# A 2:4-pruned linear layer on one core: a 256-column first weight piece, nine staged tiles in the place of ten, and a new order of the opening

## The chip, the cores and the metric

The kernel runs on one core of a Trainium2 chip. The metric is device time in microseconds (us); smaller is better. Three runs of the kernel before gave 234.03, 234.43 and 234.66 us, a median of 234.43.

## The reference

`x` is [16, 512, 1024], `w` [1024, 1024], `b` [1024], all bf16. In each group of four consecutive rows of `w`, separately for each column, the two entries of largest magnitude are kept and the others are set to zero; then `x` is multiplied with the pruned `w`, and `b` is added:

```
wg = w.reshape(256, 4, 1024); mag = abs(wg)
thr = second largest of mag in each group of four
wp = (wg * (mag >= thr)).reshape(1024, 1024)
out = einsum("bsd,df->bsf", x, wp) + b
```

The 8192 tokens make 64 tiles of 128 tokens. A tile needs 16 matmuls of 128 x 128 by 512 columns: eight slices of the inner dimension (K) for each of the two halves of the output columns.

## The kernel before

**Two ways to feed TensorE (PE).** In the main loop (lines 291 to 313) everything is at hand: the pruned weights lie in `wp_nat[h]` (h is the half of the output columns) in eight K slices in natural order, and tokens come transposed by a DMA transpose (`issue_batch`, lines 214 to 221, tiles `xTs` and `xTb`). Each tile takes 16 matmuls at line 301, and VectorE (DVE) adds the bias out of PSUM at line 207; a pair of tiles is stored at line 313. The batches are of 2, 4, and then 8 tiles.

Until the weights are pruned and laid out so, the first T = 10 tiles are worked on in pieces; this is the opening, and the change lies in it. For the first half of K (g = 0) the kernel uses the weights as they are loaded, four rows of a group side by side on a partition (`w_gh`), and transposes the tokens on PE in the matching order. For the second half (g = 1) it uses `xg1`, a DMA transpose of the second half of the T tiles' columns, and `wp_nat`.

**The opening's order** is written out by hand in the string `FRONT` (lines 231 to 240); the loop below it (lines 242 to 270) issues each token's instructions in this order, and each engine works off its own in this order. The tokens:

- `A.i`: magnitudes of weight piece i (`abs_piece`), on VectorE (line 122) or on ScalarE (ACT, line 120). `P.i`: the piece's pruning (`prep_piece`), seven VectorE instructions, lines 133 to 143; the last writes the pruned weights.
- `W`, `w`: matmuls on zeros that keep PE at work (line 108), 512 and 128 columns wide.
- `T.t`: four PE transposes of tile t's first half (line 160); `C.t`: ScalarE's copy of them to SBUF (line 165).
- `M.i.t`: the four matmuls (line 179) of piece i and tile t. Pieces 0 to 4 belong to g = 0, pieces 5 to 7 to g = 1. `X.q.t`: four matmuls of 512 columns for tile t and quarter q = 2g + h, all of its columns at once.
- `V.h.t`: ScalarE copies a finished g = 0 sum from PSUM to a stage in SBUF (line 193). `O.h.t`: VectorE adds the g = 1 sum to the stage (line 197). `B.h.t`: VectorE adds the bias (line 201), and the tile is stored when both halves are done (line 210). The stages that have no `B` in the opening are done in the main loop, three or four a tile (lines 303 to 305).
- `U.g.h.c0.c1`, `Z.g.h.c0.c1`: four copies by DMA from `w_gh` to `wp_nat` (line 150), issued by SyncE (SP) or by ScalarE. Copy j fills K slice 4g + j, which the j-th of the four matmuls of a piece reads. `L.k`: the DMA transpose of batch k, issued by SP (line 219).

PSUM has eight banks, given out in turn (`next_bank`); a bank is free again when its `V`, `O` or bias addition has read it.

**Loads.** SP issues, in this order (lines 83 to 98): half of the first weight load (256 columns), tiles 0 and 1, the weights of columns 256 to 512, tiles 4 and 5, tiles 6 and 7, columns 512 to 1024, tiles 8 and 9, the two halves of g = 1, the bias, and the transpose `xg1`. ScalarE issues the other half of the first weight load and tiles 2 and 3. Although the first load has 256 columns, it is worked on in two pieces of 128.

The functions that the diff touches:

Of the kernel before, what the change touches and what calls it, by code (L numbers as in the profile page):

```python
# [10 lines left out]
def kernel(  # L11
# [7 lines left out]
    nc = tc.nc  # L19
    P = 128  # L20
# [5 lines left out]
    K = tc.keep_in_program_order  # L26

    B, S, D = x.shape
# [3 lines left out]
    NT = NTOK // P  # L32
    FH = 512
# [2 lines left out]
    xf = x.flatten_outer_dims()  # L36
    of = out.flatten_outer_dims()

    T = 10
    NE = 8  # L40

    const = ctx.enter_context(tc.tile_pool(name="const", bufs=1))
# [10 lines left out]
    def next_bank():  # L53
        bk = nbk[0] % 8
        nbk[0] += 1
        return bk
# [1 line left out]


    wv = w.rearrange("(g p m) f -> p g m f", g=2, m=4)  # L60
    pieces = [(0, 0, 128), (0, 128, 256), (0, 256, 512), (0, 512, 768), (0, 768, 1024),
              (1, 0, 256), (1, 256, 512), (1, 512, 1024)]
    w_gh = {(g, h): const.tile([P, 4, FH], bf16, name=f"w_{g}_{h}") for g in range(2) for h in range(2)}

    def w_of(i):
        g, c0, c1 = pieces[i]
        return w_gh[(g, c0 // FH)][:, :, c0 % FH:c0 % FH + c1 - c0]

    def load_w(g, c0, c1, eng=nc.sync, m0=0, m1=4):
        dst = w_gh[(g, c0 // FH)][:, m0:m1, c0 % FH:c0 % FH + c1 - c0]  # L70
        K(eng.dma_start(dst, wv[:, g, m0:m1, c0:c1]))  # L71
# [4 lines left out]
    def load_x(ta, tb, eng=nc.sync):  # L76
        xt = const.tile([P, tb - ta, KH], bf16, name=f"xh_{ta}")
        src = xf[ta * P:tb * P, 0:KH].rearrange("(t p) c -> p t c", p=P)
        K(eng.dma_start(xt[:], src))  # L79
        for t in range(ta, tb):  # L80
            xh[t] = xt[:, t - ta, :]
# [2 lines left out]
    load_w(0, 0, 256, nc.scalar, 2, 4)  # L84
    load_x(0, 2)
    load_x(2, 4, nc.scalar)
    load_w(0, 256, 512)
    load_x(4, 6)
    load_x(6, 8)
    load_w(0, 512, 1024)  # L90
    load_x(8, 10)
    load_w(1, 0, 512)
    load_w(1, 512, 1024)
    bias_sb = const.tile([P, Dout], bf16, name="bias_sb")
# [1 line left out]

    xg1 = const.tile([P, 4, T * P], bf16, name="xg1")
    K(nc.sync.dma_start_transpose(out=xg1[:], in_=xf[0:T * P, KH:D]))

# [7 lines left out]
    def warm(n):  # L107
        K(nc.tensor.matmul(bank[7][:, :n], lhsT=zeros[:, :P], rhs=zeros[:, :n], start=True, stop=True))  # L108
# [3 lines left out]
    def abs_piece(i, on_act):  # L112
        g, c0, c1 = pieces[i]
        n = c1 - c0
        if n <= 256:
            mag = mags_pool.tile([P, 4, n], bf16, name="mag")[:]
        else:
            mag = const.tile([P, 4, n], bf16, name=f"mag_{i}")[:]
        if on_act:
            K(nc.scalar.activation(mag, w_of(i), Act.Abs))  # L120
        else:
            K(nc.vector.tensor_single_scalar(
                mag.bitcast(u16), w_of(i).bitcast(u16), 0x7FFF, op=Alu.bitwise_and))
        mags[i] = mag

    def prep_piece(i):
        g, c0, c1 = pieces[i]
        n = c1 - c0
        mag = mags.pop(i)
        magv = mag.rearrange("p (a j) f -> p a j f", j=2)  # L130
        hi = tmp.tile([P, 2, FH], bf16, name="hi")[:, :, :n]
        lo = tmp.tile([P, 2, FH], bf16, name="lo")[:, :, :n]
        K(nc.vector.tensor_tensor(hi, magv[:, :, 0, :], magv[:, :, 1, :], op=Alu.max))  # L133
        K(nc.vector.tensor_tensor(lo, magv[:, :, 0, :], magv[:, :, 1, :], op=Alu.min))  # L134
        t1 = tmp.tile([P, FH], bf16, name="t1")[:, :n]
        t2 = tmp.tile([P, FH], bf16, name="t2")[:, :n]
        K(nc.vector.tensor_tensor(t1, hi[:, 0, :], hi[:, 1, :], op=Alu.min))
        K(nc.vector.tensor_tensor(t2, lo[:, 0, :], lo[:, 1, :], op=Alu.max))
        thr = tmp.tile([P, FH], bf16, name="thr")[:, :n]
        K(nc.vector.tensor_tensor(thr, t1, t2, op=Alu.max))  # L140
        mask = tmp.tile([P, 4, FH], bf16, name="mask")[:, :, :n]
        K(nc.vector.tensor_tensor(mask, mag, thr[:, None, :].to_broadcast([P, 4, n]), op=Alu.is_ge))  # L142
        K(nc.vector.tensor_tensor(w_of(i), w_of(i), mask, op=Alu.mult))  # L143
# [11 lines left out]
    def transpose_half(t):  # L155
        own[(0, t)] = next_bank()
        xv = xh[t].rearrange("p (q m) -> p m q", m=4)
        dst = bank[own[(0, t)]][:].bitcast(bf16)[:, :4 * P].rearrange("p (m q) -> p m q", m=4)
        for m in range(4):
            K(nc.tensor.transpose(dst[:, m, :], xv[:, m, :], ident[:]))  # L160
# [5 lines left out]
        xT[t] = xt  # L166


    def mm_part(q, t, c0, c1):
        g, h = divmod(q, 2)  # L170
        if c0 == 0 and q > 0:
            own[(q, t)] = next_bank()
        dst = bank[own[(q, t)]][:, c0:c1]
        for m in range(4):
            if g == 0:
                lhs, rhs = xT[t][:, m, :], w_gh[(0, h)][:, m, c0:c1]
            else:
                lhs, rhs = xg1[:, m, t * P:(t + 1) * P], wp_nat[h][:, 4 + m, c0:c1]
            K(nc.tensor.matmul(dst, lhsT=lhs, rhs=rhs, start=c0 == 0 and m == 0, stop=c1 == FH and m == 3))  # L179
# [34 lines left out]
    def issue_batch(t0, nb):  # L214
# [6 lines left out]
            xN[t0 + j] = xt[:, :, j * P:(j + 1) * P]  # L221


    batches = [(T, 2), (T + 2, 4)] + [(t, 8) for t in range(T + 6, NT, 8)]

# [1 line left out]


    FRONT = """
        A.0 A.1 P.0 W W W W W W W W w w T.0 T.1 C.0 T.2 T.3 C.1 P.1 w M.0.0 C.2 M.0.1 T.4 C.3 T.5 M.0.2 C.4 T.6 T.7
        A.2 M.0.3 C.5 M.0.4 P.2 M.1.0 M.1.1 C.6 M.0.5 M.1.2 C.7 M.0.6 M.1.3 M.1.4 A.3 M.0.7 M.1.5 M.1.6 M.1.7 A.4
        M.2.0 P.3 M.2.1 V.0.0 M.2.2 V.0.1 M.2.3 T.8 T.9 C.8 M.2.4 M.2.5 C.9 P.4 M.2.6 A.5 M.2.7 X.0.8 V.0.2 X.0.9
        V.0.3 V.0.4 M.3.0 P.5 U.1.0.0.256 V.0.5 M.3.1 M.3.2 V.0.6 M.3.3 V.0.7 M.4.0 M.3.4 A.6 M.3.5 M.4.1 V.0.8 P.6
        U.1.0.256.512 M.4.2 V.0.9 M.3.6 M.4.3 A.7 M.3.7 M.4.4 M.4.5 M.4.6 V.1.0 P.7 U.1.1.0.512 L.0 L.1 L.2 M.4.7
        V.1.1 X.1.8 V.1.2 X.1.9 V.1.3 M.5.0 V.1.4 M.5.1 V.1.5 M.5.2 V.1.6 M.5.3 M.6.0 V.1.7 M.5.4 V.1.8 O.0.0 M.5.5
        M.6.1 V.1.9 Z.0.0.0.512 Z.0.1.0.512 B.0.0 M.5.6 O.0.1 M.5.7 M.6.2 B.0.1 M.6.3 M.6.4 O.0.2 M.6.5 O.0.3 M.6.6
        M.6.7 O.0.4 X.2.8 O.0.5 X.2.9 O.0.6 M.7.0 O.0.7 O.0.8 M.7.1 O.0.9 M.7.2 O.1.0 M.7.3 O.1.1 M.7.4 O.1.2 O.1.3
        M.7.5 O.1.4 M.7.6 O.1.5 M.7.7 O.1.6 X.3.8 B.0.2 O.1.7 X.3.9 O.1.8 O.1.9  # L240
    """
    for tok in FRONT.split():
        k, *n = tok.split(".")
        n = [int(c) for c in n]
        if k in "Ww":
            warm(FH if k == "W" else P)
        elif k == "A":
            abs_piece(n[0], n[0] not in (0, 2))
        elif k == "P":
            prep_piece(n[0])  # L250
        elif k == "T":
            transpose_half(n[0])
        elif k == "C":
            copy_half(n[0])
        elif k == "M":
            g, c0, c1 = pieces[n[0]]
            h = c0 // FH
            mm_part(2 * g + h, n[1], c0 - h * FH, c1 - h * FH)
        elif k == "X":
            mm_part(n[0], n[1], 0, FH)  # L260
        elif k == "V":
            to_stage(*n)
        elif k == "O":
            add_stage(*n)
        elif k == "B":
            add_bias(*n)
        elif k in "UZ":
            unpack(*n, nc.sync if k == "U" else nc.scalar)
        elif k == "L":
            issue_batch(*batches[n[0]])  # L270
# [20 lines left out]
    for bi, (t0, nb) in enumerate(batches):  # L291
        if bi >= 1 and bi + 2 < len(batches):
            issue_batch(*batches[bi + 2])
        for t in range(t0, t0 + nb):
            if t == NT - 1:
                last_tile(t)
                continue
            bks = (next_bank(), next_bank())
            for kt in range(KT):
                for h in range(2):  # L300
                    K(nc.tensor.matmul(bank[bks[h]][:], lhsT=xN[t][:, kt, :], rhs=wp_nat[h][:, kt, :],  # L301
                                       start=kt == 0, stop=kt == KT - 1))
            for _ in range(4 if t == T else 3):
                if later:
                    add_bias(*later.pop(0))
            j = (t - T) % 2
            if j == 0:
                o_pair = outp2.tile([P, 2, Dout], bf16, name="o_pair")
            for h in range(2):
                evac_dve(o_pair[:, j, :], h, bks[h])  # L310
            if j == 1 or t == NT - 2:
                dst = of[(t - j) * P:(t + 1) * P, :].rearrange("(j p) f -> p j f", p=P)
                K(nc.scalar.dma_start(dst, o_pair[:, :j + 1, :]))
# [1 line left out]
_INS = ['x', 'w', 'b']  # L315
_OUTS = [((16, 512, 1024), 'bfloat16')]
# [25 lines left out]
```

## Time and profile before

| | |
|---|---|
| median of three runs | 234.43 us (234.03 to 234.66) |
| the profiled execution's own time | 234.52 us |
| its span, first to last instruction | 232.7 us |
| PE busy | 227.3 us |
| DVE, ACT busy | 117.6 us, 22.7 us |
| line 301, 128 x 512 matmuls of the main loop | 161.7 + 20.8 us |
| line 179, matmuls of the opening | 18.2 + 17.5 us |
| granted clock of PE | 1.00 |
| DMA, mean over the span | 164 GB/s |

How to read the profile: a row of the timeline gives start, length, engine, line, operation, what is written and read, shape and count, and in brackets the idle time before it and what ended it. The chain that ended last is followed back from the last instruction: at each step to what released it. A matmul's length contains its way through the array; matmuls follow one another faster than that, so what counts is the distance between their starts. "q" behind an engine's name is its sequencer, which issues DMAs. The idle time of an engine that is not on the chain costs nothing. A row of the DMA issues ends with the time from issue to landing, and the busy share of the DMA is a mean over 16 engines.

The page's busy shares in 40 slices (5.8 us each) show the opening in the first seven or eight: VectorE and ScalarE are at work nearly all the time in the first four or five, and only PE from there on.

```
PE   7999999999999999999999999999999999999995
DVE  3999898969375244234334334324424423433434
ACT  3989600000000000000000000000000000000000
DMA  6996499999989401993229932597228991122222
```

### The profile page before, as it was taken

What the parts mean: (1) busy time and instruction counts of PE and PEld (TensorE: products, weight loads), DVE (VectorE), ACT (ScalarE), POOL (GpSimd) and SP (SyncE); (2) the same over time, 40 slices, a digit from 0 to 9 for tenths busy, and PEclk for the clock granted to TensorE, in tenths of its full rate; (3) what the DMA queues carried; (4) which work ended last, traced back from release to release, by engine and by line L of the source; (5) the groups of instructions that cost most, each with busy time, mean ns of one, the idle gap of its engine ahead of it and who ended that gap; (6) DMA issues with size and microseconds to landing.
All of it is one profiled execution on the core that took longest, in us unless ns stands there. A gap on an engine that the chain in (4) does not pass through costs nothing.

```text
span 232.7 us, 2893 instructions
## 1 busy us (share of the span) xinstructions
PE 227.3 (98%) x1199; PEld 114.8 (49%) x1219; DVE 117.6 (51%) x209; ACT 22.7 (10%) x38; POOL 0.7 (0%) x6
## 2 busy tenths in 40 slices
PE   7999999999999999999999999999999999999995
PEld 3878774444444444444444444444444444444443
DVE  3999898969375244234334334324424423433434
ACT  3989600000000000000000000000000000000000
POOL 1000000000000000000000000000000000000000
PEclk9999999999999999999999999999999999999999
DMA  6996499999989401993229932597228991122222
GB/s 197 350 211 145 98 197 165 229 315 289 213 215 346 152 24 66 262 236 136 90 44 254 205 130 92 112 218 216 88 90 188 158 250 65 64 93 90 90 90 90
DMA packets 76700, 38.19 MB, mean 164 GB/s; under 512 B 61840, under 2 KB 68496, under 8 KB 76688
## 3 DMA queue, kind: packets, MB, share of 16 engines
q1 hardware_dynamic: 66192, 19.86, 47.1%
q10 hardware_dynamic: 10496, 18.16, 22.4%
q8 instruction: 9, 0.15, 0.3%
q14 instruction: 3, 0.02, 0.0%
HBM read 3.67 MB, written 16.78 MB: 88 GB/s over the span
## 4 chain that ended last, share of the span: by engine, by line
PE 95%; DMA 2%; SPq 1%; issue 1%; DVE 0%
PE bank L301 78%; PE bank L179 15%; DMA xh<-in_x_dram 2%; PE bank L276 2%; PE bank L160 1%; SPq L71 0%; SPq L79 0%; DVE o_sb L286 0%
## 5 line engine op out<-in xcount | busy, mean ns | idle before, releaser
L301 PE MATMUL bank<-wp_nat,xTb 128*128 128x512 bf16 x737 | 161.7, 379 | 0.8
L207 DVE TENSOR_TENSOR o_pair<-bank,bias_sb 128x512 bf16<-128x512 f32 x106 | 68.2, 685 | 98.0 <-PE bank L301 93.6
L301 PEld LDWEIGHTS <-xTb 128*128 128x128 bf16 x752 | 73.6, 98 | 88.7
L301 PE MATMUL bank<-wp_nat,xTs 128*128 128x512 bf16 x94 | 20.8, 379 | 0.1
L179 PE MATMUL bank<-w,xT 128*128 128x256 bf16 (+2 forms) x174 | 18.2, 262 | 0.2
L179 PE MATMUL bank<-wp_nat,xg 128*128 128x256 bf16 (+1 forms) x111 | 17.5, 318 | 0.1
L201 DVE TENSOR_TENSOR o_sb<-stage,bias_sb 128x512 bf16<-128x512 f32 x20 | 13.0, 685 | 7.3 <-DMA out_dram<-o_sb 7.2
L179 PEld LDWEIGHTS <-xT 128*128 128x128 bf16 x176 | 14.5, 98 | 3.1 <-ACT xT L165 0.3
L301 PEld LDWEIGHTS <-xTs 128*128 128x128 bf16 x96 | 9.4, 98 | 11.3
L179 PEld LDWEIGHTS <-xg 128*128 128x128 bf16 x112 | 11.0, 98 | 6.4
L197 DVE TENSOR_TENSOR stage<-bank,stage 128x512 f32<-128x512 f32 x20 | 13.0, 684 | 2.0 <-PE bank L179 1.8
L193 ACT COPY stage<-bank 128x512 f32<-128x512 f32 x20 | 10.3, 681 | 0.3 <-PE bank L179 0.3
L120 ACT ACTIVATE mag<-w 128x1024 bf16<-128x1024 bf16 (+2 forms) x6 | 6.9, 1167 | 0.4 <-DMA w<-in_w_dram 0.4
L142 DVE TENSOR_TENSOR mask<-mag,thr 128x1024 bf16<-128x1024 bf16 (+2 forms) x8 | 5.5, 692 | 0.3
L143 DVE TENSOR_TENSOR w<-w,mask 128x1024 bf16<-128x1024 bf16 (+2 forms) x8 | 5.5, 692 | 0.3
L165 ACT COPY xT<-bank 128x512 bf16<-128x512 bf16 x10 | 5.2, 598 | 1.9 <-PE bank L160 1.9
L108 PE MATMUL bank<-zeros 128*128 128x512 bf16 (+1 forms) x11 | 4.0, 536 | 1.2 <-DVE zeros L101 1.2
L276 PE MATMUL bank<-wp_nat,xTb 128*128 128x128 bf16 (+2 forms) x32 | 3.7, 272 | 0.0
L160 PE MATMUL bank<-ident,xh 128*128 128x128 bf16 x40 | 3.1, 228 | 0.3 <-DMA xh<-in_x_dram 0.3
L133 DVE TENSOR_TENSOR hi<-mag 128x512 bf16<-128x512 bf16 (+2 forms) x8 | 3.4, 420 | 0.1
L134 DVE TENSOR_TENSOR lo<-mag 128x512 bf16<-128x512 bf16 (+2 forms) x8 | 3.3, 417 | 0.0
L276 PEld LDWEIGHTS <-xTb 128*128 128x128 bf16 x32 | 2.5, 98 | 1.3
(16 smaller groups left out, 16.0 us busy)
## 6 DMA issues: line engine op xcount, KB each, us to landing
out_dram<-o_pair ACTq DMA_DIRECT2D x26, 512.0 KB, 2.9
out_dram<-o_sb ACTq DMA_DIRECT2D x10, 256.0 KB, 5.3
w<-in_w_dram SPq DMA_DIRECT2D x3, 512.0 KB, 7.0
xh<-in_x_dram SPq DMA_DIRECT2D x4, 256.0 KB, 4.9
wp_nat<-w ACTq DMA_DIRECT2D x8, 128.0 KB, 4.8
wp_nat<-w SPq DMA_DIRECT2D x8, 64.0 KB, 2.1
wp_nat<-w SPq DMA_DIRECT2D x4, 128.0 KB, 4.5
xh<-in_x_dram ACTq DMA_DIRECT2D x1, 256.0 KB, 4.2
```

The source lines that it names most:

```text
L120: K(nc.scalar.activation(mag, w_of(i), Act.Abs))
L142: K(nc.vector.tensor_tensor(mask, mag, thr[:, None, :].to_broadcast([P, 4, n]), op=Alu.is_ge))
L143: K(nc.vector.tensor_tensor(w_of(i), w_of(i), mask, op=Alu.mult))
L160: K(nc.tensor.transpose(dst[:, m, :], xv[:, m, :], ident[:]))
L165: K(nc.scalar.copy(xt[:], src))
L179: K(nc.tensor.matmul(dst, lhsT=lhs, rhs=rhs, start=c0 == 0 and m == 0, stop=c1 == FH and m == 3))
L193: K(nc.scalar.copy(stage[(h, t)][:], bank[own[(h, t)]][:]))
L197: K(nc.vector.tensor_tensor(st, bank[own[(2 + h, t)]][:], st, op=Alu.add))
L201: K(nc.vector.tensor_tensor(get_o(t)[:, f], stage.pop((h, t))[:], bias_sb[:, f], op=Alu.add))
L207: K(nc.vector.tensor_tensor(o_sb[:, f], bank[bk][:], bias_sb[:, f], op=Alu.add))
L276: K(nc.tensor.matmul(bank[bk][:, :c1 - c0], lhsT=xN[t][:, kt, :], rhs=wp_nat[h][:, kt, c0:c1], start=kt == 0, stop=kt == KT - 1))
L301: K(nc.tensor.matmul(bank[bks[h]][:], lhsT=xN[t][:, kt, :], rhs=wp_nat[h][:, kt, :], start=kt == 0, stop=kt == KT - 1))
```

## The change

The first weight load is one piece of 256 columns instead of two of 128, so the pieces are seven: 0 to 3 for g = 0, 4 to 6 for g = 1. The load of tiles 4 and 5 goes ahead of the weights of columns 256 to 512 on SP's queue. T is 9, so the third load of tokens in this row has one tile, `xg1` has nine, and the first batch of the main loop has three tiles. The magnitudes of pieces 0 and 1 are VectorE's, of the others ScalarE's. A new token `N.i.t.m` issues single matmuls of a group of four. The order of the opening is new: the transposes of tiles 4 and 5 come ahead of the first real matmuls, which come after the pruning of 256 columns, and pieces 5 and 6 begin with single matmuls. No bias addition is left in the opening. At the end, tiles 61 and 62 are stored one by one, each when it is ready.

```diff
-    T = 10
+    T = 9
-    pieces = [(0, 0, 128), (0, 128, 256), (0, 256, 512), (0, 512, 768), (0, 768, 1024),
+    pieces = [(0, 0, 256), (0, 256, 512), (0, 512, 768), (0, 768, 1024),
               (1, 0, 256), (1, 256, 512), (1, 512, 1024)]
     load_x(2, 4, nc.scalar)
+    load_x(4, 6)
     load_w(0, 256, 512)
-    load_x(4, 6)
     load_x(6, 8)
     load_w(0, 512, 1024)
-    load_x(8, 10)
+    load_x(8, 9)
-    def mm_part(q, t, c0, c1):
+    def mm_part(q, t, c0, c1, ms=range(4)):
         g, h = divmod(q, 2)
-        if c0 == 0 and q > 0:
+        if c0 == 0 and q > 0 and 0 in ms:
             own[(q, t)] = next_bank()
         dst = bank[own[(q, t)]][:, c0:c1]
-        for m in range(4):
+        for m in ms:
-    batches = [(T, 2), (T + 2, 4)] + [(t, 8) for t in range(T + 6, NT, 8)]
+    batches = [(T, 12 - T), (12, 4)] + [(t, 8) for t in range(16, NT, 8)]
     FRONT = """
-        A.0 A.1 P.0 W W W W W W W W w w T.0 T.1 C.0 T.2 T.3 C.1 P.1 w M.0.0 C.2 M.0.1 T.4 C.3 T.5 M.0.2 C.4 T.6 T.7
...
+        A.0 P.0 W W W W W W W W w w T.0 T.1 C.0 T.2 T.3 C.1 w T.4 T.5 C.2 w M.0.0 A.1 C.3 M.0.1 P.1 C.4 T.6 T.7 C.5
+        M.0.2 M.0.3 C.6 M.0.4 A.2 M.0.5 M.0.6 C.7 P.2 M.1.0 A.3 M.0.7 M.1.1 A.4 M.1.2 M.1.3 V.0.0 M.1.4 M.1.5 V.0.1
+        P.3 M.1.6 V.0.2 M.1.7 V.0.3 T.8 M.2.0 C.8 M.2.1 M.2.2 V.0.4 X.0.8 V.0.5 P.4 U.1.0.0.256 V.0.6 M.2.3 M.2.4
+        A.5 M.2.5 M.3.0 V.0.7 M.3.1 V.0.8 M.2.6 P.5 U.1.0.256.512 M.3.2 V.1.0 M.2.7 A.6 M.3.3 M.3.4 M.3.5 M.3.6
+        V.1.1 M.3.7 P.6 U.1.1.0.512 L.0 L.1 L.2 V.1.2 X.1.8 V.1.3 M.4.0 V.1.4 M.4.1 V.1.5 M.4.2 M.4.3 V.1.6 M.4.4
+        V.1.7 M.4.5 N.5.0.0 V.1.8 Z.0.0.0.512 Z.0.1.0.512 M.4.6 N.5.0.1 N.5.0.2 M.4.7 N.5.0.3 M.5.1 O.0.0 M.5.2
+        O.0.1 M.5.3 M.5.4 O.0.2 M.5.5 M.5.6 O.0.3 M.5.7 O.0.4 X.2.8 O.0.5 N.6.0.0 N.6.0.1 O.0.6 N.6.0.2 N.6.1.0
+        N.6.1.1 O.0.7 N.6.0.3 N.6.1.2 N.6.1.3 M.6.2 O.0.8 O.1.0 M.6.3 O.1.1 M.6.4 O.1.2 M.6.5 O.1.3 M.6.6 O.1.4
+        O.1.5 M.6.7 O.1.6 X.3.8 O.1.7 O.1.8
     """
-            abs_piece(n[0], n[0] not in (0, 2))
+            abs_piece(n[0], n[0] >= 2)
-            if j == 1 or t == NT - 2:
-                dst = of[(t - j) * P:(t + 1) * P, :].rearrange("(j p) f -> p j f", p=P)
-                K(nc.scalar.dma_start(dst, o_pair[:, :j + 1, :]))
+            if j == 1 or t >= NT - 3:
+                j0 = j if t >= NT - 3 else 0
+                dst = of[(t - j + j0) * P:(t + 1) * P, :].rearrange("(j p) f -> p j f", p=P)
+                K(nc.scalar.dma_start(dst, o_pair[:, j0:j + 1, :]))
```

More of the change, by code (lines that the diff above doesn't have):

```diff
@@ L221, in issue_batch @@
             xN[t0 + j] = xt[:, :, j * P:(j + 1) * P]
-    batches = [(T, 2), (T + 2, 4)] + [(t, 8) for t in range(T + 6, NT, 8)]
+    batches = [(T, 12 - T), (12, 4)] + [(t, 8) for t in range(16, NT, 8)]
     FRONT = """
-        A.0 A.1 P.0 W W W W W W W W w w T.0 T.1 C.0 T.2 T.3 C.1 P.1 w M.0.0 C.2 M.0.1 T.4 C.3 T.5 M.0.2 C.4 T.6 T.7
[L233 to L240, printed above, removed]
+        A.0 P.0 W W W W W W W W w w T.0 T.1 C.0 T.2 T.3 C.1 w T.4 T.5 C.2 w M.0.0 A.1 C.3 M.0.1 P.1 C.4 T.6 T.7 C.5
[7 more added lines that the diff above has]
+        O.1.5 M.6.7 O.1.6 X.3.8 O.1.7 O.1.8
     """
@@ L244 @@
         n = [int(c) for c in n]
-        if k in "Ww":
+        if k in "MN":
+            g, c0, c1 = pieces[n[0]]
+            h = c0 // FH
+            mm_part(2 * g + h, n[1], c0 - h * FH, c1 - h * FH, n[2:] or range(4))
+        elif k in "Ww":
             warm(FH if k == "W" else P)
         elif k == "A":
-            abs_piece(n[0], n[0] not in (0, 2))
+            abs_piece(n[0], n[0] >= 2)
         elif k == "P":
@@ L254 @@
             copy_half(n[0])
[L255 to L258, printed above, removed]
         elif k == "X":
```

## The prediction, made blind

> **What bounds the kernel now.** I read the page's busy shares first, then the chain that ended last, then that chain in order of time, and last the timeline of the first 45 us, engine by engine.
>
> The page, its first section and the shares of the chain:
>
> ```profile
> PE 227.3 (98%) x1199; PEld 114.8 (49%) x1219; DVE 117.6 (51%) x209; ACT 22.7 (10%) x38; POOL 0.7 (0%) x6
> ...
> PE 95%; DMA 2%; SPq 1%; issue 1%; DVE 0%
> ```
>
> TensorE (PE) carries the chain. In order of time (start, length, what):
>
> ```profile
> 2.47 4.91 DMA xh<-in_x_dram
> 7.37 0.05 issue
> 7.42 0.64 PE bank L160 x8
> ...
> 33.33 10.09 PE bank L179 x46
> 43.42 1.73 PE bank L301 x8
> ...
> 226.45 3.51 PE bank L276 x32
> ```
>
> From 7.42 us, when the load of tiles 4 and 5 lands, to 229.96 the chain never leaves PE, and PE's timeline has no hole over 0.1 us in that stretch. So the change can act in three ways only: move the start at 7.42, change PE's sum of work behind it, or put a hole into it. PE's timeline around the start:
>
> ```profile
> 6.26 0.89 PE L179 MATMUL bank<-w,xT 128*128 128x128 bf16 x8
> 7.42 0.64 PE L160 MATMUL bank<-ident,xh 128*128 128x128 bf16 x8 [0.27 <-DMA xh<-in_x_dram]
> ...
> 8.15 0.64 PE L160 MATMUL bank<-ident,xh 128*128 128x128 bf16 x8
> ```
>
> Ahead of 7.42 PE has done T.0 to T.3 and two 128-column groups (M.0.0, M.0.1).
>
> **Pitches.** Groups of one form give start-to-start times ((length − last one) / (count − 1)): 128 columns (2.34 − 0.22)/38 = 0.056 us, 256 columns (6.71 − 0.27)/59 = 0.109, 512 columns 10.79 per 50 = 0.216, a transpose 0.056.
>
> **Step 1, where the dense stretch starts.** VectorE's chain for one piece of 256 columns, as it runs now for the third piece (first and last two rows):
>
> ```profile
> 7.76 0.42 DVE L122 TENSOR_SCALAR mag<-w 128x1024 uint16<-128x1024 uint16 x1
> 8.22 0.43 DVE L133 TENSOR_TENSOR hi<-mag 128x512 bf16<-128x512 bf16 x1
> ...
> 10.47 0.69 DVE L143 TENSOR_TENSOR w<-w,mask 128x1024 bf16<-128x1024 bf16 x1
> 11.07 0.42 DVE L133 TENSOR_TENSOR hi<-mag 128x512 bf16<-128x512 bf16 x1
> ```
>
> Start of the magnitudes to end of the multiply: 11.16 − 7.76 = 3.40 us; the next chain can begin 3.31 after, and without magnitudes on VectorE a piece takes 11.07 − 8.22 = 2.85. The first weights land as now, so A.0 starts at 3.72 and the first 256 columns are ready at 7.12; with 0.04 for the hand-over M.0.0 starts at 7.16. Transposes T.4, T.5 need load_x(4,6), which takes the second weight load's place in the queue (256 KB both): that one lands 4.6 us after its issue at 1.75, so at 6.4. T.4 and T.5 (8 x 0.056 = 0.45) then lie in 6.4 to 6.9, beside VectorE's chain, at no cost. If that load came 0.3 later, they would push M.0.0. In the order of work, 7.16 with T.4, T.5 done and M.0.0, M.0.1 open (each of these two worth 8 old instructions at 0.056) equals 7.42 before: 0.26 us gained.
>
> **Step 2, two small waits.** load_x(6,8) has the same bytes ahead of it and lands as now, for T.6 at 8.15; PE is through M.0.0 and M.0.1 at 7.16 + 2 x 0.437 = 8.03: 0.12 us of wait. The second weight load now lands where load_x(4,6) did (7.38); A.1 is moved from ScalarE to VectorE, starts at 7.42, and the piece is ready at 10.82. PE is there (M.1.0) at 8.63 + 5 x 0.437 = 10.81, so about 0.05. ScalarE's A.2 stands ahead of C.7: its 512 KB load (6.0 us after 3.63) lands at 9.6, C.7 ends near 11.25, M.0.7 comes at 11.30: covered by 0.05. Lost in all: 0.17, plus 0.03 of weight loads not hidden behind transposes.
>
> **Step 3, PE's work.** Before, 7.42 to 43.26: 24 transposes (1.34), 56 matmuls of 128 columns (3.13), 160 of 256 (17.47), 64 of 512 (13.82): 35.76, against 35.84 in the trace. After, from 7.16: 12 transposes (0.67), 192 of 256 (20.97), 48 of 512 (10.36): 32.00, and 0.20 of step 2, so the main loop begins at 39.36. It has one tile more, 16 x 0.216 = 3.45, and is level with the old main loop's start at 42.81 against 43.26. The content alone gives 0.31 (four transposes 0.22, the small matmuls 0.09).
>
> **Step 4, what is moved.** Each of these is hidden only if its deadline, now earlier, is met.
> (a) VectorE ends the second piece at 10.82 against 11.16 and all later pieces follow at the same pace, so SP's copies of g=1 are issued 0.34 earlier, the last four (U.1.1) at 27.1, 27.7, 28.35 and 29.0. PE, counted back from 39.36 (M.6 6.91 and X.3.8 0.86, then X.2.8 0.86, then M.5 and M.4 3.49 each), reaches M.6 at 31.6 (34.6 before) and M.4 at 23.7 (25.9 before). M.4.0's fourth copy is issued at 21.3 and needed at 24.1; four such copies land 2.1 after issue in the median, one took 3.4, so this is met by 0.6 or missed by 0.6. The order opens M.6 with single matmuls (N.6.0, N.6.1), so that PE can go on as each copy lands: the U.1.1 copies are needed at 31.6, 31.8, 32.05 and 32.7. Before, they took 2.9, 3.4, 5.7 and 5.9; the fourth and the batch behind it:
>
> ```profile
> wp_nat<-w SPq DMA_DIRECT2D x1, 128.0 KB, 5.9
> ...
> xTs<-in_x_dram SPq DMA_TRANSPOSE x1, 10.2
> ```
>
> With the same durations the third and fourth land at 34.05 and 34.9, and PE stands 2.0 + 0.2 = 2.2 us. With the 2.1 of the quiet time they land by 31.1 and PE stands not at all. Between: ScalarE's eight copies (Z) share the time. ScalarE has two stage copies fewer, and V.1.0 at 19.2, A.6 1.81 and six copies at 0.477 put the first Z at 24.5 against 26.12, 1.6 earlier where U.1.1 is only 0.34 earlier. Two Z copies of 128 KB are then out of its way; at the 191 GB/s that the stretch 27 to 33 moved that is 1.35 us, so 32.7 and 33.55, a wait of 0.7 + 0.2. Those two copies were also late by one of 16 engines alone: fifteen had landed 1.2 to 1.5 us before the last, which nothing in the trace ties to this order. Without it the copies are in time. I take no wait, with 0 and 2.2 kept as ends.
> The Trainium skill, page "DMA: Bandwidth & Descriptors", section "Issuing engines are not separate DMA queues", speaks against this part: DMAs issued by Scalar and Sync run on the same 16 engines and interleave, so an earlier Z helps U.1.1 only by bytes that are through before it starts. By that rule taken strictly the wait of 0.9 above stands and the sum is 235.0; the trace agrees as far as 2.1 us alone against 5.9 in company goes.
> (b) The first batch has three tiles. Now two tiles end 5.3 us after U.1.1 (35.23 to 40.55) with two Z copies beside them; the next four take 4.83 alone, 1.2 a tile. So three take 3.6 plus the 2.9 that the Z copies cost: from 32.7 to 39.2, needed at 39.36. Scaled by tile (2.65 each) it is 40.7, a wait of 1.3. I take 39.2.
> (c) One tile fewer to transpose on SP (xg1, 10.26 us for ten) frees SP near 17, while U waits for VectorE until 19.4: nothing. VectorE's additions and stores of the nine tiles lie in the 93.6 us that it waits for PE; if that cover went it would be 0.69 each. Tiles 61 and 62 stored apart are one ACT issue more (0.38), ahead of the last tile's matmuls: nothing on the path.
>
> **Sum.** 0.26 + 0.31 − 0.20 + 0.08 (the old stretch's own small gaps) = 0.45, less rounding of the hand-overs: 0.4. The profiled execution took 234.52 (span 232.73 and 1.79 around it): 234.1. It lies 0.09 above the median of the three runs (234.43), which the sum leaves aside.
>
> **Rivals.** About 0.3% (0.7 us: below 233.73 or above 235.13) is what a measurement of this kernel can tell from no change.
> R1, slower: PE, now three us earlier at M.6, waits for U.1.1's third and fourth copies as slow as today. For it: today the fourth landed at 35.23 and its matmul ran at 35.27, no slack at all. Against it: Z's head start. Price 2.2, so 234.1 + 2.2 = 236.3; it decides from a third copy later than 33.2 (1.15 us of wait).
> R2, part of the same: one late copy or the three-tile batch late by 0.4 to 1.3: 234.5 to 235.4, by its middle 234.9.
> R3, the change doesn't do what it says: the swapped load is no earlier for PE, or M.0.0's longer chain only moves the wait from before T.4 to before M.0.0; without the 0.26 and with the small waits doubled it is 234.1 + 0.26 + 0.17 = 234.5.
> R4, better: the waits of step 2 vanish and a wait ends sooner by the scatter of the loads: 234.1 − 0.2 − 0.25 = 233.65.
>
> **Numbers.** Forecast 0.45, R1 0.21, R2 0.20 (0.03 of it beyond 235.13), R3 0.05, R4 0.09. So faster 0.09, same 0.45 + 0.17 + 0.05 = 0.67, slower 0.24. The range reaches from R4 to R1, 233.7 to 236.3, and leaves out the joint case of late copies and a late batch, and R4's lower half.
>
> **What would show it.** Step 1: M.0.0 at 7.1 to 7.3 and T.4 before 6.6. Step 2: T.6 at 8.15, M.1.0 near 10.85. Step 3: main loop from 39.4. Step 4: line 179's 512-column matmuls without a hole between 31.6 and 33, and the first matmul on xTs without one at 39.4. I am wrong if PE has holes of more than 0.3 us at these two places, or if the loads land in another order than their issues.

## The result and the profile after

The changed kernel takes 236.14 us (median of 9 runs, 235.81 to 238.12) against 234.59 for the kernel before (9 runs): a ratio of 1.0089, with an interval of 1.0071 to 1.0107. The forecast of 234.1 was on the wrong side; the time lies in the range, 0.2 below what rival R1 gave (236.3). The profiled execution, the fastest of the nine, took 235.81 us and has a span of 234.0; the span of before is 232.7. Of all the runs below, one of t9_only, at 241.24 us with a granted clock of 0.986, is in the slow state and is left out of that kernel's time and ratio.

The page's shares of the chain, and the chain in order of time around the place where it leaves VectorE (start, length, what):

```profile
PE 84%; DVE 10%; DMA 3%; SPq 1%; issue 0%
```

```profile
25.60 1.24 DVE w L143
...
26.85 0.54 SPq L150
...
27.44 0.61 SPq L150
...
28.09 1.00 SPq L150
...
29.14 5.15 DMA wp_nat<-w
...
34.34 6.85 PE bank L179 x31
41.19 186.48 PE bank L301 x864
```

Before, the chain was on PE from 7.42 us on. Now it runs through VectorE's pruning of all seven pieces, to the last multiply at 26.84, then through SP's four issues of U.1.1, and through the landing of the fourth of these copies, 5.15 us after its issue. Only from 34.34 is it PE's. Nothing that PE gains ahead of 34 us can then reach the end. PE's timeline shows what it did meanwhile:

```profile
7.21 1.03 PE L179 MATMUL bank<-w,xT 128*128 128x256 bf16 x8
8.08 0.61 PE L160 MATMUL bank<-ident,xh 128*128 128x128 bf16 x8
...
23.58 8.45 PE L179 MATMUL bank<-wp_nat,xg 128*128 128x256 bf16 x70
32.83 0.81 PE L179 MATMUL bank<-wp_nat,xg 128*128 128x512 bf16 x3 [0.81 <-DMA wp_nat<-w]
34.34 6.85 PE L179 MATMUL bank<-wp_nat,xg 128*128 128x512 bf16 x31 [0.69 <-DMA wp_nat<-w]
41.02 19.16 PE L301 MATMUL bank<-wp_nat,xTs 128*128 128x512 bf16 x88
```

The same stretch in the kernel before, where line 179 runs on to the main loop without a hole:

```profile
25.91 17.51 PE L179 MATMUL bank<-wp_nat,xg 128*128 128x256 bf16 x111
43.26 7.07 PE L301 MATMUL bank<-wp_nat,xTs 128*128 128x512 bf16 x31
```

In the changed kernel the real matmuls begin at 7.21, M.4 at 23.58, and then there are two holes ahead of the matmuls that read U.1.1's third and fourth copy. By the distance of starts (1.184 and 1.072 us where 0.216 is the pitch) they are 0.97 and 0.86: 1.83 us. The main loop begins at 41.02; the old one's tile 10 began at 43.26, and a tile takes 3.45, so the loop is 1.2 us behind, the same as the difference at PE's end (231.20 against 229.98 where VectorE takes over).

### The profile page after: what moved, and what is told of

Read it like the earlier page. It is cut to its first block, busy times and chain, and to the rows that moved or that the text cites. A ratio compares the mean times of both kernels' runs of the same rounds, so it can differ in the third digit from the quotient of the medians.

```text
span 234.0 us, 2827 instructions
## 1 busy us (share of the span) xinstructions
PE 228.3 (98%) x1184; PEld 114.4 (49%) x1184; DVE 116.2 (50%) x200; ACT 20.6 (9%) x34; POOL 0.7 (0%) x6
## 4 chain that ended last, share of the span: by engine, by line
PE 84%; DVE 10%; DMA 3%; SPq 1%; issue 0%
PE bank L301 80%; PE bank L179 3%; DVE mask L142 2%; DVE w L143 2%; DMA wp_nat<-w 2%; PE bank L276 1%; DMA w<-in_w_dram 1%; DVE hi L133 1%; DVE lo L134 1%; DVE thr L140 1%; SPq L150 1%; DVE t L138 1%; DVE t L137 1%; DVE mag L122 0%; DVE o_sb L286 0%
## 5 line engine op out<-in xcount | busy, mean ns | idle before, releaser
L301 PE MATMUL bank<-wp_nat,xTs 128*128 128x512 bf16 x112 | 24.3, 379 | 0.0
L301 PEld LDWEIGHTS <-xTs 128*128 128x128 bf16 x112 | 11.0, 98 | 13.2
L179 PE MATMUL bank<-w,xT 128*128 128x256 bf16 (+1 forms) x136 | 16.2, 279 | 0.1
L201 DVE TENSOR_TENSOR o_sb<-stage,bias_sb 128x512 bf16<-128x512 f32 x18 | 11.5, 685 | 6.0 <-DMA out_dram<-o_sb 6.0
L120 ACT ACTIVATE mag<-w 128x1024 bf16<-128x1024 bf16 (+1 forms) x5 | 6.1, 1233 | 0.2 <-DMA w<-in_w_dram 0.2
L142 DVE TENSOR_TENSOR mask<-mag,thr 128x1024 bf16<-128x1024 bf16 (+1 forms) x7 | 5.4, 768 | 0.2
L143 DVE TENSOR_TENSOR w<-w,mask 128x1024 bf16<-128x1024 bf16 (+1 forms) x7 | 5.4, 768 | 0.2
L133 DVE TENSOR_TENSOR hi<-mag 128x512 bf16<-128x512 bf16 (+1 forms) x7 | 3.2, 459 | 0.1
L134 DVE TENSOR_TENSOR lo<-mag 128x512 bf16<-128x512 bf16 (+1 forms) x7 | 3.2, 456 | 0.0
L108 PEld LDWEIGHTS <-zeros 128*128 128x128 bf16 x12 | 1.5, 135 | 3.4 <-issue 2.2
```

The lines of the kernel that those rows point to most:

```text
L201: K(nc.vector.tensor_tensor(get_o(t)[:, f], stage.pop((h, t))[:], bias_sb[:, f], op=Alu.add))
```

## Experiments

Theory A: U.1.1's third and fourth copies come late because ScalarE's eight Z copies now share the DMA engines with them, and PE, which comes to M.6 three us earlier, waits for them. Its rivals: B, the loss comes from the new order of the first 25 us; D, those copies are slow of themselves; E, the single matmuls cost something. Each kernel was timed in turn with the kernel before on the same chip (three chips in all); the ratios are to that.

**t10: ten tiles again, the rest of the change kept** (tile 9's tokens put back at these places, a few groups of matmuls beside them reordered, tiles 61 and 62 stored as before the change):

```diff
-    T = 9
+    T = 10
+ T.9 behind T.8, C.9 behind C.8, X.0.9 behind M.2.2, X.1.9 behind V.1.3, X.2.9 and X.3.9 behind X.2.8 and X.3.8, V and O likewise
```

> The new opening with ten tiles instead of nine (tile 9's transposes, X, V and O tokens put back, first batch of two tiles, tiles 61 and 62 in the pairing of before); the 256-column piece, the load order and the single matmuls stay. Theory A (PE now comes to M.6 before SP's last four copies have landed, because they share the DMA engines with ScalarE's Z copies): two more 512-column groups and a set of transposes lie ahead of M.6, so PE comes 1.9 us later, at about 33.7, Z starts 0.95 later, and the wait of 1.83 us shrinks to 0 to 0.9: 234.1 to 235.0 us, and if nothing is left of the wait 0.4 below the kernel before. Rival B (the loss comes from the new order of the first 25 us): the loss stays, near 236.

234.32 us, ratio 0.9995 (0.9979 to 1.0011): the loss is gone. The profiled execution, at 235.20 among the slower of its twelve, has one hole of 0.43 (0.27 by the row) ahead of the fourth copy:

```profile
26.16 9.96 PE L179 MATMUL bank<-wp_nat,xg 128*128 128x256 bf16 x76
36.39 7.71 PE L179 MATMUL bank<-wp_nat,xg 128*128 128x512 bf16 x35 [0.27 <-DMA wp_nat<-w]
```

The copies are no earlier: the fourth lands at 36.34, 6.2 us after its issue. But PE comes 2.6 us later (M.4 at 26.16 against 23.58; the tenth tile's work is 1.9 of it) and finds them nearly there. B falls: the new front is all in this kernel.

**t9_only: nine tiles in the kernel before, nothing else:**

```diff
-    T = 10
+    T = 9
- T.9 C.9 X.0.9 X.1.9 X.2.9 X.3.9, V.0.9, V.1.9, O.0.9, O.1.9
```

> The kernel before with nine tiles instead of ten and nothing else (its pieces of 128 columns, its load order, its order without tile 9's tokens). Theory A: its fourth copy landed with no slack at all; PE now comes 1.95 us earlier to M.7, Z only 0.95 earlier, so PE waits 1 to 1.9 us at the 512-column matmuls of line 179, and the time is 235.2 to 236.2. Rival B (the loss comes from the first piece, the load order or the new order of the opening): no loss, 234.2 to 234.6.

236.85 us, ratio 1.0102 (1.0078 to 1.0125). Slower, as A said and B did not, and by more than expected. The place was another:

```profile
24.10 0.49 PE L179 MATMUL bank<-wp_nat,xg 128*128 128x256 bf16 x3
26.25 1.80 PE L179 MATMUL bank<-wp_nat,xg 128*128 128x256 bf16 x15 [1.66 <-DMA wp_nat<-w]
28.91 0.27 PE L179 MATMUL bank<-wp_nat,xg 128*128 128x256 bf16 x1 [0.86 <-DMA wp_nat<-w]
29.68 13.71 PE L179 MATMUL bank<-wp_nat,xg 128*128 128x256 bf16 x84 [0.50 <-DMA wp_nat<-w]
```

The holes lie at the 256-column copies (U.1.0), whose issue at 20.57 to 26.14 is over a microsecond behind that of the changed kernel (19.15 to 23.88). PE comes to U.1.1 so late then that it waits for nothing there. This execution, at 238.08, is over 1 us above the four others; VectorE stood 0.8 us in it behind a weight load, which made the copies later, so the holes of the others may be shorter and lie elsewhere. One tile less costs 2.4 us without the new front and 2.2 with it (1.0089 against 0.9995): by these profiles it takes away the work that covered the copies. This run speaks against B, but not for Z as the cause.

**z_late: Z held back behind X.2.8:**

```diff
- Z.0.0.0.512 Z.0.1.0.512 behind V.1.8
+ behind X.2.8: a ScalarE copy of 16 columns of its bank, then Z.0.0.0.512 Z.0.1.0.512
```

> The changed kernel with ScalarE's eight Z copies held back until X.2.8 is through PE (a 16-column ScalarE copy of its result stands ahead of them). Theory A (Z's traffic makes U.1.1 late): the four U.1.1 copies land 2.1 to 2.9 us after their issues, by 31.6, and PE has no hole at M.6; Z is then issued from 31.8 to 37, lands at 38.5 to 40.5, and the main loop, ready at 39.3, may wait for it: 234.2 to 235.4. Theory D (the copies are slow of themselves, whatever else runs): third and fourth still take over 4 us, PE waits 1.5 to 2 us at M.6 as before and then for Z: 236 to 237.5.

248.13 us, ratio 1.057. At M.6 the result is clear: no hole over 0.11 us, and the third and fourth copies landed 3.0 and 3.7 us after their issues. The rows of these two single issues in the DMA issues, first of this kernel, then of the changed one:

```profile
wp_nat<-w SPq DMA_DIRECT2D x1, 128.0 KB, 3.0
...
wp_nat<-w SPq DMA_DIRECT2D x1, 128.0 KB, 3.7
```

```profile
wp_nat<-w SPq DMA_DIRECT2D x1, 128.0 KB, 4.7
...
wp_nat<-w SPq DMA_DIRECT2D x1, 128.0 KB, 5.2
```

The issue times change too: 27.03, 27.62, 28.27 and 28.93 here, 26.85, 27.44, 28.09 and 29.14 there, where SP's third and fourth issues took 1.00 and 1.42 us instead of 0.60. So between these two kernels Z's traffic is worth 1.67 and 1.45 us of landing time to the two, and 0.4 of issue to the fourth. D holds for a part: without Z the four copies take 2.5 to 3.7 us and not the 2.1 of the 64 KB copies. The time was badly missed because Z itself came much too late:

```profile
23.63 15.89 PE L179 MATMUL bank<-wp_nat,xg 128*128 128x256 bf16 x103
39.36 0.38 PE L303 MATMUL bank<-wp_nat,xTs 128*128 128x512 bf16 x1
44.04 1.89 PE L303 MATMUL bank<-wp_nat,xTs 128*128 128x512 bf16 x4 [4.30 <-DMA wp_nat<-w]
50.54 1.01 PE L303 MATMUL bank<-wp_nat,xTs 128*128 128x512 bf16 x2 [4.61 <-DMA wp_nat<-w]
```

PE is through M.4 to X.3.8 without a longer hole and begins the main loop at 39.36, which is what the prediction had for a kernel without waits. Then it stands for Z: the last two copies were issued only at 44.73 and 45.31. The first of them began 0.03 us after the second transposed batch had landed (44.70), whose semaphore it uses again; it is one of eight semaphores that all DMAs share in turn. Waiting isn't the whole loss: after PE has stood for over four us, its granted clock is 0.5 from 43.7 to 57.4 us, and fourteen matmuls of that stretch stand 0.38 to 0.43 us apart in place of 0.216, which is 2.8 us more.

**z00_sp: the first four Z copies issued by SP, ahead of U.1.0.0:**

```diff
- Z.0.0.0.512 behind V.1.8 (ScalarE)
+ Y.0.0.0.512 ahead of P.4 U.1.0.0.256: the same four copies, issued by SP
```

> The changed kernel with the first four Z copies (Z.0.0) issued by SP between xg1 and U.1.0.0, where SP waits for VectorE; Z.0.1 stays on ScalarE. Theory A: half of Z's 1 MB is gone from the stretch 26 to 33; the third and fourth U.1.1 copies land by 31.5 to 32.7, the wait at M.6 falls from 1.83 to 0 to 0.4: 234.1 to 234.6, and never over the kernel before by more than 0.2. Theory D (copies slow of themselves) or a fixed delay by SP's semaphores: unchanged, near 236.

234.20 us, ratio 0.9987 (0.9975 to 0.9998), by the ratios over 2 us below the changed kernel, and 0.3 below the one before. SP issues these copies from 15.72 to 18.7, where it waited for VectorE. U.1.1's third and fourth copies landed at 32.52 and 32.87, 3.4 and 3.1 us after their issues; the third is only 0.27 earlier than in the changed kernel, because SP's second issue took 1.43 us and put it off, the fourth 1.42. PE's timeline:

```profile
23.99 16.07 PE L179 MATMUL bank<-wp_nat,xg 128*128 128x256 bf16 x103
39.89 22.39 PE L301 MATMUL bank<-wp_nat,xTs 128*128 128x512 bf16 x101
```

One gap of 0.29 is left in the first row, before the third copy's matmul at 32.56. This execution was at 234.69 the slower end of twelve; its M.0.0 began at 7.62 (see the last section), 0.4 later than in the changed kernel's profile, which hides as much of the wait.

**z_early: all of Z ahead of U.1.1** (Z.0.1 from ScalarE behind A.6, near 20 us):

```diff
- Z.0.1.0.512 behind V.1.8
+ Z.0.1.0.512 behind A.6, with Y.0.0.0.512 as above
```

> As z00_sp, and the other four Z copies (Z.0.1) issued by ScalarE right behind A.6, near 20 us, so that no Z traffic is left when U.1.1 starts. Theory A: third and fourth U.1.1 copies land 2.1 to 3.7 us after their issues, by 30.7 and 32.0, no hole at M.6; but Z.0.1 now shares 21 to 25 with U.1.0, whose fourth copy is needed at 24.0: a hole of 0 to 0.8 at M.4 may take its place. 233.9 to 234.8, by its middle 234.1; the main loop starts no later than in z00_sp unless that hole is there.

235.81 us, ratio 1.0053 (1.0040 to 1.0067): no hole at M.6, to which PE comes over 1 us later than in z00_sp, but a larger one than expected ahead of M.4, and not for U.1.0's copies. PE's timeline, then ScalarE's:

```profile
25.08 16.04 PE L179 MATMUL bank<-wp_nat,xg 128*128 128x256 bf16 x104 [1.31 <-ACT stage L193]
```

```profile
20.83 3.57 ACTq L150 DMA_DIRECT2D wp_nat<-w  x4
24.44 4.01 ACT L193 COPY stage<-bank 128x512 f32<-128x512 f32 x8 [3.04 <-DVE thr L140]
```

With no Z beside them U.1.1's third and fourth copies landed at 32.13 and 32.48, 3.9 and 3.6 us after their issues: earlier than the 32.79 and 34.29 of the changed kernel, but later than the 30.7 and 32.0 expected. ScalarE's eight stage copies stood 3.04 us behind the four issues, and M.4.0 needs a bank that one of them frees. Each issue began 0.02 to 0.08 us after another copy had landed (20.75, 21.68, 22.86, 23.82 against 20.83, 21.70, 22.88, 23.85) whose semaphore it uses again. The row's releaser (DVE) had long been done; the landing is what ended it.

**z_all_sp: all of Z on SP,** Z.0.1 between U.1.0.256 and U.1.1:

```diff
- Z.0.1.0.512 behind V.1.8 (ScalarE)
+ Y.0.1.0.512 ahead of P.6 U.1.1.0.512 (SP), with Y.0.0.0.512 as above
```

> z00_sp with the other four Z copies (Z.0.1) on SP too, between U.1.0.256 and U.1.1, so that ScalarE issues none and its copies wait for no semaphore. SP issues them from 24.7 to 27.3, U.1.1 starts 0.3 later than in z00_sp. Theory A with one queue only: the copies land in the order of issue, the third and fourth U.1.1 by 32.0 and 32.7, holes 0 to 0.5: 234.0 to 234.6. Rival (two queues at once slow each other more than their bytes do): clearly better than z00_sp, no hole, 234.0.

235.13 us, ratio 1.0021 (1.0008 to 1.0035): worse than z00_sp, and short of the expectation. U.1.1 was issued at 29.06 to 30.98 instead of 27.06 to 29.77 in z00_sp, behind the four Z copies, one of which took 1.55 us to issue; its last two copies landed 2.8 and 2.9 us after their issues, at 33.13 and 33.89. So the copies were quicker and were issued later; the queue of one issuer is a limit of its own here.

**n6_off: the single matmuls of M.6 taken out:**

```diff
- N.6.0.0 N.6.0.1 O.0.6 N.6.0.2 N.6.1.0 N.6.1.1 O.0.7 N.6.0.3 N.6.1.2 N.6.1.3
+ M.6.0 O.0.6 M.6.1 O.0.7
```

> The changed kernel without the single matmuls of M.6: the four matmuls of tile 0, then the four of tile 1. Theory A (PE stands until the third and the fourth copy have landed, whatever it could do meanwhile): only the two matmuls of tile 1 that ran between the two waits come behind the second one, 2 x 0.216 us: 0.4 above the changed kernel. Rival E (the single matmuls themselves cost something, a changed order of weight loads or banks): faster than the changed kernel.

236.51 us, ratio 1.0097 (1.0072 to 1.0122), against 1.0081 (1.0062 to 1.0101) for the changed kernel on the same chip. The two intervals overlap so far that neither the 0.4 us nor E (faster without them) is decided: inconclusive.

**after_same: the changed kernel again:**

> The changed kernel again, unaltered, beside the others on one chip. Theory A: 235.8 to 237.3, and where a profile is longer, the excess lies in the same two holes ahead of the third and fourth U.1.1 copies.

236.50 us (235.76 to 237.03). This profile, at 236.86, is 1.05 above the first one, and so are its holes:

```profile
33.01 0.81 PE L179 MATMUL bank<-wp_nat,xg 128*128 128x512 bf16 x3 [0.74 <-DMA wp_nat<-w]
35.38 6.85 PE L179 MATMUL bank<-wp_nat,xg 128*128 128x512 bf16 x31 [1.56 <-DMA wp_nat<-w]
```

By starts they are 0.26 (at the second copy), 0.90 and 1.72, in all 2.88 against 1.83: 1.05 more. The fourth copy landed at 35.33, 6.1 after its issue, instead of 34.29. So the difference of these two executions has its place at these copies, the fourth above all. That the scatter of all runs of the changed kernel, some near 235.9 and some near 237, lies there too is likely, but not shown.

**x_old and z00_x_old: the old order of the two loads,** in the changed kernel and in z00_sp:

```diff
-    load_x(4, 6)
     load_w(0, 256, 512)
+    load_x(4, 6)
```

> The changed kernel with its two loads back in the old order on SP (weights of columns 256 to 512 ahead of tiles 4 and 5). PE then starts M.0.0 near 7.9 instead of 7.2. Theory A (the main loop's start is set by the landing of the fourth U.1.1 copy, not by PE's start): the 0.7 us are taken from the two holes at M.6, the main loop starts at the same time and the time is that of the changed kernel, 235.8 to 236.5. Rival (PE's start is worth its full length): 236.5 to 237.2.

> z00_sp (the first four Z copies on SP ahead of U.1.0.0) with the two loads in the old order. Here the copies come nearly in time (holes of 0.3 us in all), so PE's later start should be paid for, less that 0.3: 0.3 to 0.6 above z00_sp, 234.5 to 234.8. Rival (the start is covered by something else as well): no difference, 234.2.

The changed kernel with this edit: 236.45 us, ratio 1.0070 (1.0046 to 1.0094), not above the changed kernel's 1.0089 and 1.0081. z00_sp with it: 234.89, ratio 1.0008 (0.9997 to 1.0020), some 0.5 us above z00_sp's 0.9987. PE's timeline of the first of the two:

```profile
7.98 1.04 PE L179 MATMUL bank<-w,xT 128*128 128x256 bf16 x8
...
33.36 0.81 PE L179 MATMUL bank<-wp_nat,xg 128*128 128x512 bf16 x3 [0.57 <-DMA wp_nat<-w]
35.20 6.85 PE L179 MATMUL bank<-wp_nat,xg 128*128 128x512 bf16 x31 [1.03 <-DMA wp_nat<-w]
41.88 20.45 PE L301 MATMUL bank<-wp_nat,xTs 128*128 128x512 bf16 x94
```

PE starts 0.77 later than in the changed kernel, and its main loop, at 41.88, lies between those of the changed kernel's two profiles (41.02 and 42.06): the same edit is free where the copies bound, and costs half a microsecond where they hardly do. That is the strongest evidence for one half of A, that the copies' landing and not PE's arrival sets the time. That Z's traffic makes them late rests on z_late, z_early and z00_sp.

## Why the prediction was wrong

*Step 1 was right.* Forecast M.0.0 at 7.16, measured 7.21; T.4 at 6.4, measured 6.43.

*Step 2 was right in kind.* T.6 came at 8.08 (8.15 forecast), and line 179 shows no hole over 0.05 us up to M.4.

*Step 3 was right.* M.4 began at 23.58 (23.7 forecast). Without its two holes the main loop would have begun at 41.02 − 1.83 = 39.19, forecast 39.36; in z_late, where the holes are all but absent, it began at 39.36. z00_sp, with a hole of 0.29, comes to −0.3 us against the kernel before, where the sum said −0.4 for no hole.

*Step 4 (a) failed.* It put PE's wait for U.1.1's third and fourth copies at nothing; the wait was 1.83 us. Its own working gave 32.7 and 33.55 for the two landings and a wait of 0.9; they came at 32.79 and 34.29. The prediction then took neither this nor the row of before (2.2), but "no wait", because it reckoned the fast end, 2.1 us for a copy, as reachable and one engine's lateness as accidental. Neither reason held. The 2.1 are of 64 KB copies, and 128 KB copies take 2.5 to 3.9 us even without Z (z_late and z_early). And the lateness wasn't one engine's: eight of the 16 parts of the fourth copy landed at 34.0 to 34.3, where before fifteen had landed by 33.72 and one at 35.23. Nor did Z's head start suffice, though Z began earlier than forecast (23.84 against 24.5). The nearest row was that of the same copies in the same company, and it was the better guide. A smaller term was left out: SP's third and fourth issues took 1.00 and 1.42 us against 0.60, so the fourth copy was issued at 29.14. What makes an issue long isn't shown; in the kernel before, one of a 64 KB copy took 1.25 us with none of ScalarE's copies under way.

The rule cited there, from the Trainium skill, page "DMA: Bandwidth & Descriptors", section "Issuing engines are not separate DMA queues", agrees with the runs: copies issued by SP slow from 3.0 and 3.7 us to 4.7 and 5.2 when ScalarE's run beside them. The comparison made there, 2.1 us against 5.9, was of 64 KB with 128 KB. Taken strictly, with a wait of 0.9 and 235.0 us, it would have given the right side, with half of the wait.

*Step 4 (b) was pessimistic, without effect.* The three-tile batch landed at 37.34 (39.2 forecast), since Z was through by 34.52. *Step 4 (c)* held: no other place shows a wait of PE.

*The rivals.* R1 is what happened: the same place, the same two copies, 1.83 us of its 2.2. The 1.15 us of wait by which it was to be told were passed, but not as it said: the third copy landed at 32.79, ahead of its 33.2, and the fourth brought 0.86 us in place of 0.2. With a slack of 0.04 us in the row of before, its chance of 0.21 was low. R2's batch, R3 and R4 did not come.

*What stays open.* Why the fourth copy lands at 34.3 in one execution of the changed kernel and at 35.3 in another; its 16 engines' parts land over 1.5 us in the one (32.74 to 34.29) and 2.5 in the other (32.84 to 35.33). What makes some of SP's issues take 1.00 to 1.55 us in place of 0.60. And how much of the 2.5 to 3.9 us without Z is the transposed batch's, which SP issues right behind the fourth copy: no run moves it.

## What to carry to other kernels

Work taken away ahead of a transfer's deadline is worth only the slack that the transfer has: here the fourth copy landed 0.04 us before its matmul, so three us of earlier arrival had to come out of somewhere, and the row that prices it is the same transfer beside the same traffic, not a faster one from a quiet time. Look for copies that can go before the crowded stretch on an issuer that stands idle (SP from 16 to 19 us here): moving four of them gave over 2 us, more than the whole change was to bring. And put no DMA issue ahead of an engine's own work where its semaphore may still be in use.

## What the runs showed of the hardware that was not expected

In these kernels an issue of a DMA waits for the landing of the last transfer that used the same semaphore. With eight semaphores in turn for both queues this ties ScalarE's issues to SP's landings: in z_early it held ScalarE's copies for 3.04 us, in z_late it put off Z's seventh copy to 44.73.

The moment from which PE runs at full pace is not the same in each execution: the 16 transposes of T.0 to T.3 are spaced 0.056 us apart from 5.42 on in the kernel before and 0.107 all through to 7.05 in the profile of z00_sp, whose first row reads

```profile
5.36 1.86 PE L160 MATMUL bank<-ident,xh 128*128 128x128 bf16 x16 [0.36 <-DMA xh<-in_x_dram]
```

against 1.24 for the same transposes before. In the changed kernel they are through in 1.32 us (5.05 to 6.37), here in 1.69 (5.36 to 7.05), and M.0.0 came at 7.62 though its weights were ready at 6.90. The mean granted clock of the profile is 1.00 in both stretches, because it counts the time ahead of the clock's first record as full; this record lies at 5.41 us in the kernel before, at 5.96 in the changed kernel and at 7.06 in z00_sp, where the spacing changes. The Trainium skill, page "TensorE: Matmul & The Clock Gate", section "Part 1: The HAM clock gate (the "warmup" mystery)", has it that the window that decides on the clock runs freely, so that the switch comes at another point in each run. The three profiles agree with that, but the 1.65 us between the earliest and the latest are more than the 0.5 us either way that it gives.

The clock also falls within a kernel: in z_late, where PE stood from 39.7 to 44.0 us, it is 0.5 from 43.7 on, and PE comes back to full pace only at 57.4, behind two more waits.
